# Packing the last 96 gate and up columns of two slabs in each gated layer, with another order of loads at the start

## Chip, cores, metric

One Trainium2 chip, one of its cores. The metric is the device time of one execution, in microseconds. The kernel before takes 395.33 us (median of three runs, 395.28 to 396.86).

## The reference

Four residual layers on x of 2048 tokens by 512 features, bf16: A, B, A, B, each on a layer norm of x, with the same weights in both A and both B.

```python
def _A_ref(x, wqkv, w_phi, wo):            # H = 32 heads of Dh = 16
    q, k, v = split(x @ wqkv)
    pq = einsum("bhsd,hdf->bhsf", q, w_phi); pk = einsum("bhsd,hdf->bhsf", k, w_phi)
    phi_q = concat([softmax(pq), softmax(-pq)]); phi_k = concat([softmax(pk), softmax(-pk)])
    kv = einsum("bhsf,bhsd->bhfd", phi_k, v);  z = einsum("bhsf->bhf", phi_k)
    o = einsum("bhqf,bhfd->bhqd", phi_q, kv) / (einsum("bhqf,bhf->bhq", phi_q, z)[..., None] + 1e-6)
    return heads_joined(o) @ wo

def _B_ref(x, W_gate, W_up, W_down):       # 512 -> 1376 -> 512
    gate = x @ W_gate; up = x @ W_up
    return ((gate * (gate > 0)) * up) @ W_down

x = x + _A_ref(layernorm(x)); x = x + _B_ref(layernorm(x))
x = x + _A_ref(layernorm(x)); x = x + _B_ref(layernorm(x))
```

## The kernel before

**Tiles and slabs.** The 2048 tokens are 16 tiles of 128, or 4 slabs of 512. x stays on the chip (`x_sb`); every layer norm writes a normalized tile, which is transposed into `yT` (features on the partitions, in 4 pieces of 128), by a DMA, or for the first four tiles by TensorE and a copy.

**Attention layer.** w_phi is folded into the query and key weights (`compose_k`, `compose_q`): the wqkv key columns are loaded in four row pieces (wk0 to wk3 below), transposed on TensorE (L514), copied (L518, L520), multiplied with a block-diagonal form of w_phi (`BD`, built by GpSimd at L495 from `phi_c` and `mask8`), and copied to `Wkp` (L524). Then `kv_proj` or `kv_pair` for each tile: keys and values by matmul, two exps on ScalarE, the key sums Zk (L634) and their reciprocal (L636) on VectorE, the division on GpSimd (L639), and `kv_acc`, which adds up phi_k times v over all tiles in banks 0 to 2. `kv_fin` brings this to SBUF; `num` makes each tile's numerator and denominator (L711), divides (VectorE and GpSimd), transposes by DMA, and multiplies with wo (L742).

**Gated layer.** F = 1376 columns are eleven chunks: ten of 128 and one of FLAST = 96. For a group of tiles (`ts`: two tiles, or a slab of four), `glu_up` does per chunk four gate matmuls and four up matmuls (one for each 128 features; n = 256 or 512 tokens stream through a stationary of 128 or 96 columns), L763, then ReLU of the gate by ScalarE into one of three gate buffers (L765), and the product with the up half into one of NHU = 18 buffers of `hT`: by VectorE straight from PSUM (L775), or, for the chunks in `on_act`, through a copy of the up half by ScalarE (L770) and a product from SBUF (L772). `glu_down` (L790) multiplies, for each tile, the eleven chunks of hT with Wd into one bank, the 96-row chunk last, and VectorE adds the result to x (L792). In the first gated layer slabs 2 and 3 go without `on_act`, and their steps are mixed with numerators and the next attention layer's keys; in the last one all chunks are in `on_act`, and slabs 2 and 3 have no other work mixed in.

**Order.** No engine's order is written by hand. The program is a list of operations with what they read and write, an estimated duration, and for DMAs a number of bytes. A planner (`schedule`) places them: at each step the operation that can start first, ties broken by a priority, within a window of operations per engine (24 on GpSimd, 40 on VectorE, 64 on ScalarE, 400 on TensorE). It does so 48 times with different priorities and keeps the order with the shortest end by its own durations. So a changed duration or byte count can alter the order anywhere. Operations with a `boost` (all loads of the start) are first on their queue, in the order in which they are written. On the chip each engine then runs its list in order and waits by semaphores. All matmuls of a PSUM bank and their readers are ordered by the bank (`RP`).

**The start.** SP issues x tile 0, phi, tiles 1 to 3, then (after wk2 has landed, `first`) tiles 4 and 5, 6 and 7, wv, 8 to 11, 12 to 15, and the transposed load of the query weights; ScalarE's queue issues wk0 to wk3. Tiles 0 to 3 are transposed through banks 7, 0, 1 and 0; the key and value banks of layer A0 cycle through 4, 5, 6, 7 (tile 0: 4 and 5, tile 1: 6 and 7). The weights wo, Wg, Wu and Wd are loaded later by SP, after yT of tile 15.

Of the kernel before, what the change touches and what calls it, by code (L numbers as in the profile page):

```python
# [347 lines left out]
ALU = mybir.AluOpType  # L348
# [7 lines left out]
NHU = 18  # L356
# [12 lines left out]
class Kernel:  # L369
# [27 lines left out]
    def alloc(self, E):  # L397
        nc = self.nc

        def sb(name, shape, dt=BF16):  # L400
            t = E(nc.sbuf_tensor(name, [P] + shape, dt))
            setattr(self, name, t)
            return t

        sb("x_sb", [NT, 512])
        sb("yT", [NC, S])
        sb("wv_p", [NC, 512])
        sb("Wqp", [NC, 512])
        sb("Wkp", [NC, 512])
        sb("wo_p", [NC, 512])  # L410
        sb("Wg", [NC, F])
        sb("Wu", [NC, F])
        sb("Wd", [NFC, 512])
        sb("expk", [NT, 2, 512])
        sb("vsb", [NT, NC, 130])
        sb("expq", [NSLAB, NC, 2, 512])
        sb("kvbd", [NG, GW])
        sb("hT", [NHU, 512])
        sb("numbf", [2, NG, GW])
        sb("tsc", [2, 1024])  # L420
        sb("osb", [2, 512])
        sb("oT", [4, NC, 128])
        sb("gate_sb", [3, 512])
        sb("ytile", [4, 512])
        sb("ident", [128])
        sb("mask8", [8])
        sb("mask8t", [8])
        sb("phi_c", [NC, DH])
        sb("stats6", [NT, 6], FP32)
        sb("mv", [NT, 2], FP32)  # L430
        sb("rv1", [NT, 1], FP32)
        sb("rstd", [NT, 1], FP32)
        sb("nmr", [NT, 1], FP32)
        sb("agg", [4, 3], FP32)
        sb("aggw", [2], FP32)
        sb("mhalf", [4, 1], FP32)
        sb("Zk", [2, 64], FP32)
        sb("rZk", [4, 64], FP32)
        sb("zm", [2, 64], FP32)
        sb("zd", [2, 32], FP32)  # L440
        sb("zr", [2, 32], FP32)
        sb("ab", [2, 64])
        self.ps = E(nc.psum_tensor("ps", [P, 8, 512], FP32))
        self.pb = [self.ps[:, i, :] for i in range(8)]
        self.RP = [self.r("pb", i) for i in range(8)]


    def setup(self):
        op, dma, r = self.op, self.dma, self.r
        k = self  # L450
# [16 lines left out]
           [r("tsc", 0)], [r("mask8t")], 200, "mask8 a")  # L467
        op("pool", lambda e: e.affine_select(k.mask8[:], k.mask8t[:], [[16, 8]], ALU.is_ge, 0.0, base=15, channel_multiplier=-1),
           [r("mask8t")], [r("mask8")], 200, "mask8 b")
# [3 lines left out]
        def ldx(t0, t1, after=()):  # L473
            dma("sp", lambda e: e.dma_start(k.x_sb[:, t0:t1, :], xv[:, t0:t1, :]), list(after), [r("x", t) for t in range(t0, t1)], 96000 if t1 == t0 + 1 else (131072 if t0 < 8 else 86000) * (t1 - t0), f"dma x{t0}")
        ldx(0, 1)
        dma("act", (lambda ic: lambda e: e.dma_start(wk_n[:, ic, :], A_wqkv[ic * 128:(ic + 1) * 128, 512:1024]))(0), [], [R_wkn[0]], 96000, f"dma wk0")
        dma("sp", lambda e: e.dma_start(k.phi_c[:], A_w_phi.rearrange("(kc hl) d f -> (hl d) kc f", hl=8)), [], [r("phi_c")], 16384, "dma phi")
        dma("act", (lambda ic: lambda e: e.dma_start(wk_n[:, ic, :], A_wqkv[ic * 128:(ic + 1) * 128, 512:1024]))(1), [], [R_wkn[1]], 96000, f"dma wk1")
        ldx(1, 2)
        dma("act", (lambda ic: lambda e: e.dma_start(wk_n[:, ic, :], A_wqkv[ic * 128:(ic + 1) * 128, 512:1024]))(2), [], [R_wkn[2]], 96000, f"dma wk2")  # L480
        ldx(2, 3)
        dma("act", (lambda ic: lambda e: e.dma_start(wk_n[:, ic, :], A_wqkv[ic * 128:(ic + 1) * 128, 512:1024]))(3), [], [R_wkn[3]], 96000, f"dma wk3")
        ldx(3, 4)
        first = [R_wkn[2]]
        ldx(4, 6, first)
        ldx(6, 8, first)
        dma("sp", lambda e: e.dma_start(k.wv_p[:], wqkv_v[:, :, 1024:1536]), first, [r("wv", ic) for ic in range(NC)], 345000, "dma wv")
        ldx(8, 12, first)
        ldx(12, 16, first)
        o = dma("sp", lambda e: e.dma_start_transpose(WqT, A_wqkv[:, 0:512]), first, R_WqT, 422000, "dma wqT")  # L490
        o.dur = 6400.0
        for j, o in enumerate(self.prog.ops[n0:]):
# [6 lines left out]
           [r("phi_c"), r("mask8")], [R_BD], 1040, "BD")  # L499
# [248 lines left out]
    def glu_up(self, ts, ring, tag, out, on_act=()):  # L748
# [29 lines left out]
        for fc in range(NFC):  # L778
            out.append(lambda fc=fc: step(fc))

# [21 lines left out]
    def emit(self):  # L802
        from itertools import cycle
        self.unit, self.unit_of = 0, {}
# [4 lines left out]
        for t in tiles(0):  # L809
            self.ln(t, "L0", pe_bank=(7, 0, 1, 0)[t], copy_act=True)  # L810
# [23 lines left out]
        for i, piece in enumerate(pieces):  # L834
            piece(self.r("yT", 15 if i < 8 else 15))
        kv(6, 2)
# [7 lines left out]
        for li in (0, 2):  # L844
# [11 lines left out]
            def steps_B(ts, on_act=()):  # L856
                out = []
                self.glu_up(ts, gring, B, out, on_act)
# [6 lines left out]
            def steps_N(ts):  # L865
                return [lambda t=t: N([t]) for t in ts]
# [29 lines left out]
            if not last:  # L896
                mix(steps_B(tiles(2)), steps_N([14, 15]) + steps_K(0))
                mix(steps_B(tiles(3)), steps_K(1) + steps_K(2) + [lambda: self.q_proj(0, mring, "A2")])
# [7 lines left out]
            else:  # L906
                mix(steps_B(tiles(2), HA), [])
                mix(steps_B(tiles(3), HA), [])
# [68 lines left out]
```

## Time and profile before

| what | us |
|---|---|
| median of three runs | 395.33 |
| the profiled execution | 395.28 |
| its span, first to last instruction | 393.6 |

Busy time of the engines in it, us, by stretches of the span:

| stretch | what runs | PE | DVE | ACT | POOL |
|---|---|---|---|---|---|
| 0 to 20 | loads, composed weights, first tiles | 13.21 | 12.37 | 12.55 | 9.65 |
| 20 to 54 | rest of the first keys and values | 31.52 | 31.12 | 27.18 | 32.65 |
| 54 to 75 | queries, first numerators | 19.49 | 16.42 | 18.27 | 8.27 |
| 75 to 225 | first gated layer, mixed with both neighbours | 149.16 | 113.58 | 63.37 | 67.71 |
| 225 to 275 | second attention layer's turn | 48.44 | 38.29 | 36.19 | 24.74 |
| 275 to 375 | second gated layer | 99.47 | 51.02 | 45.65 | 26.09 |
| 375 to 393.6 | its end | 15.93 | 5.29 | 4.45 | 0.00 |

In the lines of the profile, PE is TensorE's matmuls, PEld its weight loads, DVE VectorE, ACT ScalarE, POOL GpSimd, SPq the issuing of DMAs by SyncE. A matmul's duration includes a tail that runs under the next one, so the distance between two starts is its cost in a stream. The granted TensorE clock was 1.00 throughout the span.

### The profile page before, as it was taken

The numbers are of one execution on the slowest core, as the hardware profiler recorded it, in microseconds if no ns is written. First come the engines' busy times: TensorE is split into PE (matmuls) and PEld (weight loads), VectorE is DVE, ScalarE is ACT, GpSimd is POOL, SyncE is SP. The second block draws the span as 40 slices with busy tenths as digits, with TensorE's granted clock in tenths as the row PEclk, the third lists the DMA queues.
The fourth block names the chain that finished last, engine by engine and source line by source line (L and its number), as shares of the span: only waits on it lengthen the run. The fifth ranks groups of instructions, "written<-read, shape, count | busy, mean of one in ns | idle before, by whom it ended". The sixth has DMA issues, their size and how long they took to land.

```text
span 393.6 us, 6346 instructions
## 1 busy us (share of the span) xinstructions
PE 377.2 (96%) x2288; PEld 208.1 (53%) x2331; DVE 268.1 (68%) x547; ACT 207.7 (53%) x389; POOL 169.1 (43%) x284
## 2 busy tenths in 40 slices
PE   4899899999999999999999999989999999999997
PEld 3345464676744444444444457467774454444444
DVE  4799878887757899866756867877775567322322
ACT  4789759743734312543454474985464562454340
POOL 5499934552543373364344543474544152100000
PEclk9999999999999999999999999999999999999999
DMA  6933681322220312301000010142322132100001
GB/s 166 222 68 82 182 305 40 55 53 43 55 40 13 55 41 57 80 14 28 13 13 2 20 36 2 40 68 54 68 55 60 35 51 58 40 2 27 28 13 53
DMA packets 61679, 23.01 MB, mean 58 GB/s; under 512 B 53488, under 2 KB 60624, under 8 KB 61648
## 3 DMA queue, kind: packets, MB, share of 16 engines
q1 hardware_dynamic: 60928, 22.02, 24.6%
q10 hardware_dynamic: 720, 0.59, 0.5%
q8 instruction: 18, 0.29, 0.3%
q14 instruction: 13, 0.11, 0.1%
HBM read 7.91 MB, written 2.10 MB: 25 GB/s over the span
## 4 chain that ended last, share of the span: by engine, by line
PE 84%; DVE 5%; DMA 4%; issue 4%; ACT 1%; SPq 0%; ACTq 0%; POOL 0%; DVEq 0%; POOLq 0%
PE ps L763 39%; PE ps L790 19%; PE ps L622 8%; PE ps L742 6%; PE ps L695 6%; PE ps L711 4%; PE ps L668 3%; DMA x_sb<-in_A_x_dram 2%; DVE rZk L636 1%; DMA yT<-ytile 1%; DVE stats L556 1%; DMA hT<-in_A_wqkv_dram 1%; DVE Zk L634 1%; DVE ytile L599 0%; ACT expq L698 0%
## 5 line engine op out<-in xcount | busy, mean ns | idle before, releaser
L763 PE MATMUL ps<-yT,Wg 128*128 128x512 bf16 (+3 forms) x436 | 125.9, 336 | 1.4 <-ACT expk L770 0.7
L763 PE MATMUL ps<-yT,Wu 128*128 128x512 bf16 (+3 forms) x435 | 123.8, 336 | 0.4
L765 ACT ACTIVATE gate_sb<-ps 128x512 bf16<-128x512 f32 (+3 forms) x110 | 56.2, 512 | 108.3 <-PE ps L763 94.3
L790 PE MATMUL ps<-Wd,hT 128*128 128x512 bf16 (+2 forms) x351 | 104.4, 372 | 0.6
L639 POOL TENSOR_TENSOR expk<-expk,rZk 128x1024 bf16<-128x1024 bf16 (+1 forms) x32 | 59.5, 1882 | 29.6 <-DVE rZk L636 21.0
L763 PEld LDWEIGHTS ps<-yT,Wg 128*128 128x128 bf16 (+1 forms) x440 | 43.7, 100 | 34.3 <-issue 1.3
L763 PEld LDWEIGHTS ps<-yT,Wu 128*128 128x128 bf16 (+1 forms) x440 | 43.8, 100 | 33.3 <-DVE hT L775 0.2
L790 PEld LDWEIGHTS ps<-Wd,hT 128*128 128x128 bf16 (+1 forms) x363 | 35.3, 98 | 36.0 <-DVE x_sb L792 0.4
L772 DVE TENSOR_TENSOR hT<-gate_sb,expk 128x512 bf16<-128x512 bf16 (+3 forms) x73 | 28.9, 396 | 31.3 <-ACT expk L770 30.6
L556 DVE BATCH_NORM_STATS2 stats<-x_sb 128x6 f32<-128x512 bf16 x64 | 42.3, 675 | 7.9 <-DMA x_sb<-in_A_x_dram 7.6
L634 DVE TENSOR_REDUCE Zk<-expk 128x64 f32<-128x1024 bf16 x32 | 37.9, 1202 | 9.3 <-ACT expk L625 9.3
L366 ACT ACTIVATE numbf<-ps 128x432 bf16<-128x432 f32 x64 | 33.1, 541 | 16.5 <-PE ps L711 16.2
L736 POOL TENSOR_TENSOR osb<-tsc 128x512 bf16<-128x512 bf16 x28 | 33.0, 1178 | 20.2 <-DVE tsc L731 18.0
L742 PE MATMUL ps<-wo_p,oT 128*128 128x512 bf16 x122 | 38.1, 379 | 0.7 <-DMA oT<-osb 0.5
L563 POOL TENSOR_SCALAR rv<-mv 128x1 f32<-128x1 f32 (+1 forms) x53 | 12.7, 244 | 56.8 <-DVE mv L558 56.7
L770 ACT ACTIVATE expk<-ps 128x512 bf16<-128x512 f32 (+3 forms) x73 | 36.1, 495 | 0.4 <-PE ps L763 0.2
L698 ACT ACTIVATE expq<-ps 128x1024 bf16<-128x1024 f32 (+1 forms) x40 | 32.2, 866 | 5.6 <-PE ps L695 5.2
L792 DVE TENSOR_TENSOR x_sb<-x_sb,ps 128x512 bf16<-128x512 bf16 (+1 forms) x33 | 21.9, 666 | 19.2 <-PE ps L790 18.9
L625 ACT ACTIVATE expk<-ps 128x512 bf16<-128x512 f32 x44 | 23.9, 595 | 20.9 <-PE ps L622 20.6
L711 PE MATMUL ps<-kvbd,expq 128*128 128x144 bf16 x256 | 34.1, 226 | 0.5 <-ACT numbf L366 0.4
L775 DVE TENSOR_TENSOR hT<-gate_sb,ps 128x512 bf16<-128x512 bf16 (+2 forms) x37 | 22.6, 612 | 16.5 <-PE ps L763 14.4
L695 PE MATMUL ps<-yT,Wqp 128*128 128x512 bf16 x121 | 32.8, 379 | 0.8 <-ACT expq L698 0.5
(73 smaller groups left out, 442.6 us busy)
## 6 DMA issues: line engine op xcount, KB each, us to landing
out_dram<-x_sb SPq DMA_DIRECT2D x15, 128.0 KB, 1.7
Wg<-in_B_W_gate_dram SPq DMA_DIRECT2D x4, 344.0 KB, 4.9
Wu<-in_B_W_up_dram SPq DMA_DIRECT2D x4, 344.0 KB, 5.4
Wd<-in_B_W_down_dram SPq DMA_DIRECT2D x5, 256.0 KB, 7.2
x_sb<-in_A_x_dram SPq DMA_DIRECT2D x2, 512.0 KB, 7.4
yT<-ytile SPq DMA_TRANSPOSE x60, 2.4
x_sb<-in_A_x_dram SPq DMA_DIRECT2D x4, 128.0 KB, 4.6
hT<-in_A_wqkv_dram ACTq DMA_DIRECT2D x4, 128.0 KB, 3.9
```

The lines of the kernel that those rows point to most:

```text
L366: return e.activation(out, in_, ACT.Copy) if hasattr(e, "activation") else e.tensor_copy(out, in_)
L556: op("dve", (lambda t: lambda e: e.bn_stats(k.stats6[:, t, :], k.x_sb[:, t, :]))(t), [r("x", t)], [r("st", t)], 685, f"{tag} stats {t}")
L634: op("dve", lambda e: e.tensor_reduce(k.Zk[:, zb, :], k.expk[:, t, :, :].rearrange("p s (h f) -> p (s h) f", f=16), AX.X, ALU.add), [r("ex ...
L639: op(eng, (lambda s0, s1: lambda e: e.tensor_tensor(k.expk[:, t, s0:s1, :].rearrange("p s (h f) -> p (s h) f", f=16), k.expk[:, t, s0:s1, ...
L695: op("pe", (lambda c, ic, bank: lambda e: e.matmul(k.pb[bank][:], k.Wqp[:, ic, c * 128:(c + 1) * 128], k.yT[:, ic, st * 512:(st + 1) * 512 ...
L711: op("pe", (lambda s, c, j, g0, bank: lambda e: e.matmul(k.pb[bank][:, j * GW:(j + 1) * GW], k.expq[:, st, c, s, tt * 128:(tt + 1) * 128], ...
L736: op(sm, lambda e: e.tensor_tensor(k.osb[:, b, :], k.tsc[:, b, 0:512], k.tsc[:, b, 512:1024], ALU.add), [r("tsc", b)], [r("osb", b)], 418 ...
L742: op("pe", (lambda c, bank: lambda e: e.matmul(k.pb[bank][:], k.oT[:, ob, c, :], k.wo_p[:, c, :], start=(c == 0), stop=(c == NC - 1)))(c, ...
L763: op("pe", (lambda bank, W, ic, fc, Mf: lambda e: e.matmul(k.pb[bank][0:Mf, 0:n], W[:, ic, fc * 128:fc * 128 + Mf], k.yT[:, ic, c0:c0 + n] ...
L765: op("act", (lambda Mf, gb, gs: lambda e: e.activation(k.gate_sb[0:Mf, gs, 0:n], k.pb[gb][0:Mf, 0:n], ACT.Relu))(Mf, gb, gs), [self.RP[gb] ...
L770: op("act", (lambda Mf, ub, tu: lambda e: e.activation(k.expk[0:Mf, tu, 0, 0:n], k.pb[ub][0:Mf, 0:n], ACT.Copy))(Mf, ub, tu), [self.RP[ub] ...
L790: op("pe", (lambda fc, Kf, u, c0, bank, m0, m1: lambda e: e.matmul(k.pb[bank][:, m0:m1], k.hT[0:Kf, u, c0:c0 + 128], k.Wd[0:Kf, fc, m0:m1] ...
```

## The change

Two things. **Packing:** for slabs 2 and 3 of each gated layer, the last 96 gate and 96 up columns are computed from a new tensor `Wr`, which holds, per 128 features, 64 up columns, 64 gate columns, 32 up columns and 32 gate columns. GpSimd fills it once by four copies. `short64` runs the 64 + 64 as one stationary of 128 columns (4 matmuls for each slab). `short32` runs the 32 + 32 as a stationary of 64 columns; slab 2 goes to the lower half of a bank's partitions, slab 3 to the upper half, matmuls alternating (8 matmuls for both slabs, emitted as one operation after slab 2's other steps). ReLU and product run on each part by itself, straight from PSUM; the parts come together in rows 0 to 63 and 64 to 95 of one hT buffer, so `glu_down` is unchanged. Slab 3's buffer is taken when slab 2's halves run.

**The start:** phi is issued first, then tiles 0 to 3; the gate for the later loads is wk3 instead of wk2; tiles 4 to 7 are one load; the planner's byte counts for the loads are larger; tiles 0 and 1 are transposed through bank 7, 2 and 3 through bank 6. `mask8t` and `phi_c` lose their own tensors and lie in `tsc` and `hT`.

```diff
+        sb("Wr", [NC, 192])
-        sb("mask8t", [8])
-        sb("phi_c", [NC, DH])
+        self.mask8t = self.tsc[:, 1, 0:8]
+        self.phi_c = self.hT[:, 13, 0:NC * DH].rearrange("p (c f) -> p c f", c=NC)
...
-            dma("sp", ..., 96000 if t1 == t0 + 1 else (131072 if t0 < 8 else 86000) * (t1 - t0), f"dma x{t0}")
-        ldx(0, 1)
...
-        ldx(3, 4)
-        first = [R_wkn[2]]
-        ldx(4, 6, first)
-        ldx(6, 8, first)
-        dma("sp", lambda e: e.dma_start(k.wv_p[:], wqkv_v[:, :, 1024:1536]), first, ..., 345000, "dma wv")
+            dma("sp", ..., 131072 * (t1 - t0) if t1 > t0 + 1 else 96000, f"dma x{t0}")
+        dma("sp", lambda e: e.dma_start(k.phi_c[:], ...), [], [r("hT", 13)], 16384, "dma phi")
+        for ic in range(NC):
+            dma("act", ..., [], [R_wkn[ic]], 96000, f"dma wk{ic}")
+        for t in range(4):
+            ldx(t, t + 1)
+        first = [R_wkn[3]]
+        ldx(4, 8, first)
+        dma("sp", lambda e: e.dma_start(k.wv_p[:], wqkv_v[:, :, 1024:1536]), first, ..., 524288, "dma wv")
         ldx(8, 12, first)
         ldx(12, 16, first)
-        o = dma("sp", ..., first, R_WqT, 422000, "dma wqT")
-        o.dur = 6400.0
+        o = dma("sp", ..., first, R_WqT, 524288, "dma wqT")
+        o.dur = 7000.0
...
+    def pack_weights(self):
+        op, r, k = self.op, self.r, self
+        for W, nm, o0, o1 in ((k.Wu, "Wu", 0, 128), (k.Wg, "Wg", 64, 160)):
+            for dst, src, n in ((o0, 1280, 64), (o1, 1344, 32)):
+                op("pool", (lambda W, dst, src, n: lambda e: e.tensor_copy(k.Wr[:, :, dst:dst + n], W[:, :, src:src + n]))(W, dst, src, n),
+                   [r(nm, ic) for ic in range(NC)], [r("Wr", dst)], 200 + 4 * n, f"pack {nm} {dst}")
...
-    def glu_up(self, ts, ring, tag, out, on_act=()):
+    def glu_up(self, ts, ring, tag, out, on_act=(), short=0):
...
+        def short64():
+            bank = next(ring)
...
+            for ic in range(NC):
+                op("pe", (lambda ic: lambda e: e.matmul(k.pb[bank][:, 0:n], k.Wr[:, ic, 0:128], k.yT[:, ic, c0:c0 + n], start=(ic == 0), stop=(ic == NC - 1)))(ic), ...)
+            op("act", lambda e: e.activation(k.gate_sb[0:64, gs, 0:n], k.pb[bank][64:128, 0:n], ACT.Relu), ...)
+            op("dve", lambda e: e.tensor_tensor(k.hT[0:64, u, 0:n], k.gate_sb[0:64, gs, 0:n], k.pb[bank][0:64, 0:n], ALU.mult), ...)
+
+        def short32():
+            bank = next(ring)
+            t2 = list(range(ts[-1] + 1, ts[-1] + 1 + len(ts)))
+            us = [self.unit_of[ts[0], NFC - 1][0], self.new_short(t2)]
+            self.short_of[t2[0]] = us[1]
+            def mm(e):
+                for ic in range(NC):
+                    for v in range(2):
+                        last = e.matmul(k.pb[bank][v * 64:v * 64 + 64, 0:n], k.Wr[:, ic, 128:192], k.yT[:, ic, c0 + v * n:c0 + v * n + n], start=(ic == 0), stop=(ic == NC - 1), skip_group_check=True)
+                return last
+            op("pe", mm, ..., 4 * du + 190, f"{tag} Wr2 {ts[0]}")
+            for v, u in enumerate(us):
+                gs = u % 3
+                op("act", ... e.activation(k.gate_sb[64:96, gs, 0:n], k.pb[bank][v * 64 + 32:v * 64 + 64, 0:n], ACT.Relu) ...)
+                op("dve", ... e.tensor_tensor(k.hT[64:96, u, 0:n], k.gate_sb[64:96, gs, 0:n], k.pb[bank][v * 64:v * 64 + 32, 0:n], ALU.mult) ...)
+
-        for fc in range(NFC):
+        for fc in range(NFC - 1 if short else NFC):
             out.append(lambda fc=fc: step(fc))
+        if short:
+            out.append(short64)
+        if short == 2:
+            out.append(short32)
...
-            self.ln(t, "L0", pe_bank=(7, 0, 1, 0)[t], copy_act=True)
+            self.ln(t, "L0", pe_bank=(7 if t < 2 else 6), copy_act=True)
...
+        self.pack_weights()
         kv(6, 2)
...
-                mix(steps_B(tiles(2)), steps_N([14, 15]) + steps_K(0))
-                mix(steps_B(tiles(3)), steps_K(1) + steps_K(2) + [lambda: self.q_proj(0, mring, "A2")])
+                mix(steps_B(tiles(2), (), 2), steps_N([14, 15]) + steps_K(0))
+                mix(steps_B(tiles(3), (), 1), steps_K(1) + steps_K(2) + [lambda: self.q_proj(0, mring, "A2")])
...
-                mix(steps_B(tiles(2), HA), [])
-                mix(steps_B(tiles(3), HA), [])
+                mix(steps_B(tiles(2), HA, 2), [])
+                mix(steps_B(tiles(3), HA, 1), [])
```

## The prediction

> **What bounds the kernel now.** Four views, in this order: the page's busy shares, the busy time by stretches, the chain of waits of the first 45 us, and the single shapes of the lines that the change touches.
>
> ```profile
> PE 377.2 (96%) x2288; PEld 208.1 (53%) x2331; DVE 268.1 (68%) x547; ACT 207.7 (53%) x389; POOL 169.1 (43%) x284
> ```
>
> By stretches (start:end, length, busy us and instructions of PE, PEld, DVE, ACT, POOL, then clock, DMA share, GB/s):
>
> ```profile
> 20.00:30.00 10.00, 9.50 (x66) 4.98 (x66) 10.00 (x14) 8.78 (x13) 9.59 (x14) 1.00 0.36 72
> 30.00:40.00 10.00, 9.89 (x69) 5.50 (x70) 10.00 (x15) 9.03 (x12) 10.00 (x6) 1.00 0.38 82
> 40.00:50.00 10.00, 8.18 (x61) 4.63 (x61) 8.09 (x11) 7.09 (x11) 10.00 (x6) 1.00 0.72 202
> ...
> 150.00:175.00 25.00, 24.89 (x116) 11.57 (x116) 19.91 (x41) 10.90 (x20) 11.59 (x19) 1.00 0.25 50
> ...
> 200.00:225.00 25.00, 24.89 (x116) 11.50 (x117) 17.64 (x25) 11.38 (x21) 11.29 (x10) 1.00 0.03 6
> ...
> 325.00:350.00 25.00, 24.89 (x115) 11.40 (x116) 11.18 (x25) 10.66 (x20) 3.59 (x8) 1.00 0.15 37
> ```
>
> The kernel has two regimes. Until some 54 us VectorE and GpSimd set the pace: both are full from 20 to 40 us, and TensorE has 1.8 us without work in the ten after that. In the gated layers TensorE is busy 24.89 of 25 us, and no other engine is near that: there a TensorE slot saved is time saved, and work added elsewhere costs nothing until it delays TensorE. The start's pace comes from this chain (start, length, what):
>
> ```profile
> 1.73 4.75 DMA hT<-in_A_wqkv_dram
> ...
> 6.49 0.38 SPq L474
> ...
> 7.95 7.04 DMA x_sb<-in_A_x_dram
> ...
> 17.52 2.97 DVE stats L556 x5
> 20.50 1.19 DVE Zk L634 x2
> ...
> 41.90 3.29 DMA yT<-ytile
> ```
>
> The third piece of wqkv (wk2) lands at 6.48 us and lets SP issue the later tiles; tiles 8 to 11 go out at 7.95 and land at 14.99; from there VectorE runs without a pause to the last normalized tile, which TensorE awaits at 45.2. VectorE had waited 2.59 us for those tiles.
>
> **The change, part by part.** *1. Fewer matmul slots.* In slabs 2 and 3 of a gated layer the last 96 columns cost 2 x (4 gate + 4 up) = 16 matmuls. The timeline gives their slot:
>
> ```profile
> 349.58 0.38 PE L763 MATMUL ps<-yT,Wg 128*96 128x512 bf16 x1
> 349.80 0.38 PE L763 MATMUL ps<-yT,Wu 128*96 128x512 bf16 x1
> 350.01 0.38 PE L763 MATMUL ps<-yT,Wg 128*96 128x512 bf16 x1
> 350.23 0.38 PE L763 MATMUL ps<-yT,Wu 128*96 128x512 bf16 x1
> ```
>
> Start to start is 0.65/3 = 0.216 us although each lasts 0.379: 0.163 is tail, hidden under the next. So 16 slots are 3.45 us a layer. After: 64 + 64 columns in one stationary, 4 matmuls in each slab, 8 ordinary slots, 1.73 us. The 32 + 32 columns are 8 matmuls of 64 columns, alternating between two halves of the array. No row shows halves working at once, so I bound it. Perfect pairs: 4 slots, 0.86 us. Pairs with an exposed tail when the halves come into use and when they go: 0.86 + 2 x 0.163 = 1.19. No overlap, with the two tails: 1.73 + 0.33 = 2.05. A tail after each matmul: 8 x 0.379 = 3.03. Against the 1.73 that these 8 replace, the gain per layer is 0.86, 0.54, -0.33 or -1.30; for two layers 1.73, 1.07, -0.65 or -2.61. I take 1.07: the halves write different partitions and read different columns of yT, so no data orders them, and the tail is what a row shows for an array that is not refilled at once.
>
> The weight loads could break the pairs. A 128-column load takes 98 ns, a 96-column one 123 (below); two per pair make 0.20 to 0.25 us against a slot of 0.216, so at worst (0.246 - 0.216) x 4 x 2 = 0.24 us in all, kept for the range.
>
> ```profile
> L763 PEld LDWEIGHTS ps<-yT,Wg 128*96 128x96 bf16 x40 | 4.8, 123 | 3.1
> L765 ACT ACTIVATE gate_sb<-ps 96x512 bf16<-96x512 f32 x6 | 3.6, 593 | 5.3 <-PE ps L763 4.5 <-DVE tsc L731 0.8
> L775 DVE TENSOR_TENSOR hT<-gate_sb,ps 96x512 bf16<-96x512 bf16 x2 | 1.4, 684 | 1.4 <-PE ps L763 1.4
> ```
>
> Two rules of the Trainium skill speak against the edit. "TensorEngine Tiling (Array Packing)", Key Properties, says that a change of tiling mode drains the array; the tail of 0.163 us is my row for a drain, and without that rule the sum would gain 1.73 instead of 1.07. "TensorE: Matmul & The Clock Gate", Part 3, gives three column tiles a speed-up of 2.38; scaled to two tiles (an estimate from that page) it is 1.59, so 8 matmuls in 1.09 us, and a gain of 1.28 before drains; the same rows that I have show no such pair.
>
> *2. More evacuation.* Both ReLU and product now run on the 64-row and the 32-row part separately: 4 of each per layer where there were 2. A narrow tile is no cheaper (593 ns at 96 rows, 598 at 128). First layer: ACT + 2 x 0.593 = 1.19 us, DVE + 2 x 0.684 = 1.37. Second layer: four ReLUs replace two ReLUs and two copies of the up half, ACT even; DVE 4 x 0.684 - 2 x 0.416 = + 1.90. I cost all of it at nothing: in those stretches DVE has at least 5 us of every 25 free, ACT 13. If the cover went, down's eleventh matmul would wait for ReLU and product after the halves, 1.28 us; ten matmuls of the same tile, 2.16 us, stand before it.
>
> *3. Packing the weights.* Four copies on GpSimd, once. The nearest rows are the 64-element copy of 0.24 us (L503) and the 512-element product of 1.04 (L495); at 256 and 128 elements, 0.24 to 1.04 each, 1.0 to 4.2 us in all, some 1.8 in between. Wg and Wu, issued up to 47.8 us, land by 54.0; GpSimd then has a hole:
>
> ```profile
> 52.51 1.50 POOL L639 TENSOR_TENSOR expk<-expk,rZk 128x512 bf16<-128x512 bf16 x1 [0.94 <-DVE rZk L636]
> 61.41 0.31 POOL L722 TENSOR_TENSOR zm<-numbf 128x64 f32<-128x64 bf16 x1 [7.41 <-DVE numbf L366]
> ```
>
> 7.4 us hold all four: cost nothing. Put ahead of the last key normalization instead, they would wait for the weights, and kv_acc, kv_fin and every numerator behind that: up to 1.5 us and the copies.
>
> *4. The start goes over to another order.* Phi is issued ahead of tile 0: phi some 0.45 us earlier, tile 0 as much later. Neither decides: GpSimd's product with phi ends at 5.45, but the weight columns behind it wait for wk2 anyway; tile 0's statistics end at 4.3, and its tile is written at 8.0. What decides is SP's queue. The gate moves from wk2 (6.48) to wk3, whose transposes start at 7.20: + 0.72. Tiles 4 to 7 are one issue instead of two: - 0.48. Then wv, tiles 8 to 11, 12 to 15 and the transposed load follow + 0.24 later, and landings between + 0.24 and, if the queue's bytes simply slide, + 0.72. VectorE has no slack behind them: + 0.48, the middle. Below nothing too: a planner that expects tiles 8 to 11 later (524288 bytes for wv instead of 345000) may put the first two key sums (1.2 us each) into VectorE's 2.59 us wait, up to - 2.4.
>
> *5. Banks.* Tiles 2 and 3 are transposed through bank 6, tiles 0 and 1 through bank 7. Bank 6 is also where tile 1's keys go, so these now wait for tile 3's copy, which ended at 17.84 while the keys of tile 1 were done by 12.8. Zero, because tile 1's key sum runs only at 21.6; the rival below prices the rest.
>
> Sum, against the profiled execution (span 393.6, 395.28 in all; the median is 395.33): 395.28 - 1.07 + 0.48 = **394.7 us**.
>
> **Rivals.** *The start is filled better.* The key sums move into the 2.59 us wait. For it: the exps of tiles 0 and 1 end at about 13.0 and at 13.96, so the sums could run. Against: tiles 4 to 7 arrive later too, which narrows the hole. With one sum gained (1.2) and perfect pairs: 395.28 - 1.73 + 0.48 - 1.2 = 392.8.
>
> *The halves do not overlap and each matmul shows its tail.* Place: the 8 half matmuls of each layer. Price: + 2.61, so 395.28 + 2.61 + 0.48 = 398.4. It is slower by 0.5% once a half matmul costs over (1.73 + (2.03 - 0.48)/2)/8 = 0.31 us (397.31, the upper bound of no change below, is 2.03 above 395.28). For it: the weight load runs longer for narrow stationaries. Against: the 96-column matmuls keep the 0.216 slot.
>
> *Tile 1's keys stick behind bank 6.* If ScalarE keeps its order, its exps of tile 1 slide from 12.9 (four run in a row from 11.89 to 13.96) to 17.84 + 4 x 0.216 = 18.7, 5.8 us, of which its idle time from 10 to 20 us (2.1) swallows part: 3.7 us of everything behind it, 395.28 - 1.07 + 3.7 = 397.9. It decides when tile 3's copy ends after some 16 us. Against: the planner sees this dependency and can bring tile 3 forward.
>
> *The change does nothing here:* no overlap, tails only at the ends, 395.28 + 0.65 + 0.48 = 396.4, inside "no change".
>
> **How the numbers follow.** A measurement of this kernel tells 0.5%, 1.98 us, from no change; around 395.33 that is 393.35 to 397.31. Forecast 0.46 and the idle change 0.10 lie inside; better start 0.20, below; tails 0.10 and bank 6 0.14, above. So faster 0.20, same 0.56, slower 0.24. The range goes from 392.8 (perfect pairs and one sum gained, with the 0.24 of slow loads still inside) to 397.9 (the price of bank 6): beyond lie the tails' rival, 0.10, and the far halves of the other two, some 0.10.
>
> **What would show it.** Right: in slabs 2 and 3 four 64-column matmuls start in some 0.43 us, not 0.86; TensorE's busy time falls by about 1 us in the gated layers; the pack copies stand between 54 and 61 us; tiles 8 to 11 land at 15.2 to 15.7; the last key normalization ends near 54.5. Wrong: half matmuls 0.216 or 0.38 apart; key sums ahead of the statistics of tile 8; exps of tile 1 after 17 us; a GpSimd wait on Wu; or a stretch after 75 us in which TensorE falls under 24.8 of 25.

## The result, and the profile after

The changed kernel takes 393.66 us (median of six runs, 393.24 to 394.04) beside 395.35 for the kernel before: ratio 0.9951, 95% interval 0.9935 to 0.9967. Repeated later, twelve runs gave 394.99 (394.04 to 396.38) beside 395.34: ratio 0.9991, interval 0.9978 to 1.0003. In some executions of these kernels the granted TensorE clock was 0.987 to 0.996 instead of 1.00, and in six of the eight kernels that had such executions they took 1.3 to 2.2 us longer at the median; where that matters, the median of the executions at 0.999 or 1.00 is given as "at full clock". At full clock the repeat took 394.44 us (seven runs) beside 395.33. So the change is between 0.1 and 0.5% faster, within what a measurement of this kernel tells from no change. The profiled execution took 393.43 us, span 391.7, which is 1.9 below the span before.

The page's busy shares, and busy time by stretches (columns as before):

```profile
PE 375.1 (96%) x2290; PEld 205.4 (52%) x2331; DVE 270.7 (69%) x551; ACT 208.3 (53%) x391; POOL 169.9 (43%) x288
```

```profile
20.00:30.00 10.00, 8.09 (x58) 4.37 (x58) 10.00 (x13) 8.41 (x12) 8.92 (x13) 1.00 0.44 57
30.00:40.00 10.00, 9.89 (x72) 5.62 (x73) 10.00 (x13) 7.97 (x11) 10.00 (x6) 1.00 0.35 79
40.00:50.00 10.00, 8.13 (x58) 4.39 (x57) 7.89 (x10) 7.02 (x12) 10.00 (x6) 1.00 0.72 224
...
200.00:225.00 25.00, 24.89 (x115) 11.35 (x116) 17.33 (x28) 11.29 (x20) 11.95 (x11) 1.00 0.08 16
...
300.00:325.00 25.00, 24.45 (x129) 12.00 (x131) 15.71 (x33) 11.96 (x24) 9.23 (x18) 1.00 0.18 39
325.00:350.00 25.00, 24.89 (x119) 11.17 (x119) 10.92 (x25) 11.44 (x20) 2.41 (x6) 1.00 0.17 41
```

From 200 to 225 and from 325 to 350 us TensorE is as full as before, 24.89 of 25 us, and no wait of TensorE names the added ReLUs, products or copies: they are hidden. From 300 to 325 us it is not: 24.45 instead of 24.84, with a wait for a product of a slab that is not packed:

```profile
322.77 0.39 PE L840 MATMUL ps<-Wd,hT 96*128 96x512 bf16 x1 [0.39 <-DVE hT L776]
```

At the start VectorE is as full as before, but GpSimd has 1.1 us free between 20 and 30 us, and TensorE 1.9, where before they had 0.4 and 0.5. That is a place where the change lost part of what its start had won.

The timeline of TensorE around the set of halves in the last gated layer, and the shapes of the new lines:

```profile
348.48 0.81 PE L767 MATMUL ps<-yT,Wu 128*128 128x512 bf16 x3
349.22 1.05 PE L807 MATMUL ps<-yT,Wr 128*64 128x512 bf16 x8
350.20 0.39 PE L840 MATMUL ps<-Wd,hT 128*128 128x512 bf16 x1
```

```profile
L814 DVE TENSOR_TENSOR hT<-gate_sb,ps 32x512 bf16<-32x512 bf16 x4 | 2.7, 682 | 2.0 <-ACT gate_sb L812 2.0
...
L812 ACT ACTIVATE gate_sb<-ps 32x512 bf16<-32x512 f32 x4 | 2.4, 588 | 0.5 <-DVE hT L776 0.5
L807 PE MATMUL ps<-yT,Wr 128*64 128x512 bf16 x16 | 2.1, 385 | 0.0
...
L807 PEld LDWEIGHTS ps<-yT,Wr 128*64 128x64 bf16 x16 | 0.7, 109 | 1.3 <-issue 0.8
```

Three matmuls start at 348.48, 0.216 apart, the last at 348.91, so the set could start at 349.13 (348.91 + 0.216). It starts at 349.22, 0.09 later, and the next matmul stands at 350.20: 0.98 us for eight, of which four slots of 0.216 are 0.86. With the entry the set costs some 1.08 us, five slots, where eight ordinary ones would cost 1.73. Narrow tiles are not cheaper for the other engines: 588 ns for a ReLU of 32 rows, 682 for a product.

The chain of waits at the start, and the issue of tiles 8 to 15 by SP:

```profile
1.86 4.12 DMA x_sb<-in_A_x_dram
...
10.78 2.38 DVE stats L552 x4
...
15.72 4.16 DVE stats L552 x7
...
39.70 1.10 DVE ytile L593
...
43.61 3.44 DMA yT<-ytile
```

```profile
7.20 1.06 SPq L475 DMA_DIRECT2D x_sb<-in_A_x_dram  x2
```

Before, the chain held the transfer of tiles 8 to 11 (7.04 us, to 14.99). Now it holds tile 0's transfer and then VectorE and GpSimd: tiles 8 to 11 are issued at 7.20 instead of 7.95, and nothing waits for them. VectorE's and GpSimd's timelines show what took the place of that wait (columns: start, length; in brackets idle time before it):

```profile
13.36 1.18 DVE L630 TENSOR_REDUCE Zk<-expk 128x64 f32<-128x1024 bf16 x1
14.46 0.68 DVE L552 BATCH_NORM_STATS2 stats<-x_sb 128x6 f32<-128x512 bf16 x1
...
21.32 1.96 DVE L593 TENSOR_SCALAR ytile<-x_sb,rstd,nmr 128x512 bf16<-128x512 bf16 x1
```

```profile
21.21 1.93 POOL L635 TENSOR_TENSOR expk<-expk,rZk 128x1024 bf16<-128x1024 bf16 x1
...
23.90 1.93 POOL L635 TENSOR_TENSOR expk<-expk,rZk 128x1024 bf16<-128x1024 bf16 x1 [0.55 <-DVE rZk L632]
25.78 1.05 POOL L577 TENSOR_TENSOR rstd<-rv,mhalf 128x4 f32<-128x4 f32 x1
...
51.52 2.77 POOL L635 TENSOR_TENSOR expk<-expk,rZk 128x512 bf16<-128x512 bf16 x2 [1.39 <-DVE rZk L632]
54.24 0.63 POOL L748 COPY Wr<-Wg 128x256 bf16<-128x256 bf16 x2
```

The planner put tile 0's key sum into the former wait, so GpSimd divides from 21.21 on. Before, it divided from 23.45 to 51.58 without a break:

```profile
23.45 28.13 POOL L639 TENSOR_TENSOR expk<-expk,rZk 128x1024 bf16<-128x1024 bf16 x15
```

Now layer-norm operations and waits stand between the divisions, and the last one ends at 54.29 (51.52 + 2.77) against 54.01. A lead of 2.24 us became a delay of 0.28. Some of the lead was kept even so: the first matmul of the gated layers starts 0.98 us earlier than before. Before, then after:

```profile
74.95 0.27 PE L763 MATMUL ps<-yT,Wg 128*128 128x256 bf16 x1 [0.19 <-DMA yT<-ytile]
```

```profile
73.97 0.27 PE L767 MATMUL ps<-yT,Wg 128*128 128x256 bf16 x1 [0.17 <-DMA yT<-ytile]
```

So of the 1.9 us of span 0.98 come ahead of this matmul and 0.9 behind it.

### The profile page after: what moved, and what is told of

It is laid out like the page before. It is cut to its first block, busy times and chain, and to the rows that moved or that the text cites. A ratio compares the mean times of both kernels' runs of the same rounds, so it can differ in the third digit from the quotient of the medians.

```text
span 391.7 us, 6354 instructions
## 1 busy us (share of the span) xinstructions
PE 375.1 (96%) x2290; PEld 205.4 (52%) x2331; DVE 270.7 (69%) x551; ACT 208.3 (53%) x391; POOL 169.9 (43%) x288
## 4 chain that ended last, share of the span: by engine, by line
PE 81%; DVE 7%; issue 4%; DMA 3%; POOL 2%; ACT 2%; SPq 0%; DVEq 0%; POOLq 0%
PE ps L767 36%; PE ps L840 19%; PE ps L618 8%; PE ps L691 6%; PE ps L738 6%; PE ps L707 4%; PE ps L664 2%; DVE stats L552 2%; ACT expq L694 2%; DMA yT<-ytile 2%; DVE Zk L630 1%; DVE rZk L632 1%; POOL rstd L560 1%; DVE ytile L593 1%; DMA x_sb<-in_A_x_dram 1%
## 5 line engine op out<-in xcount | busy, mean ns | idle before, releaser
L767 PE MATMUL ps<-yT,Wu 128*128 128x512 bf16 (+3 forms) x419 | 117.3, 334 | 0.5 <-DVE zr L722 0.2
L767 PE MATMUL ps<-yT,Wg 128*128 128x512 bf16 (+3 forms) x415 | 114.9, 334 | 1.2 <-DMA oT<-osb 0.6
L769 ACT ACTIVATE gate_sb<-ps 128x512 bf16<-128x512 f32 (+3 forms) x106 | 53.0, 509 | 102.6 <-PE ps L767 89.7
L840 PE MATMUL ps<-Wd,hT 128*128 128x512 bf16 (+3 forms) x355 | 104.4, 373 | 0.9 <-DVE hT L776 0.4
L767 PEld LDWEIGHTS ps<-yT,Wu 128*128 128x128 bf16 (+1 forms) x424 | 42.0, 99 | 31.9 <-ACT expk L774 0.4
L767 PEld LDWEIGHTS ps<-yT,Wg 128*128 128x128 bf16 (+1 forms) x424 | 41.4, 99 | 32.0 <-issue 1.0
L774 ACT ACTIVATE expk<-ps 128x512 bf16<-128x512 f32 (+3 forms) x71 | 35.0, 495 | 8.4 <-PE ps L767 8.1
L691 PE MATMUL ps<-yT,Wqp 128*128 128x512 bf16 x123 | 34.0, 379 | 0.9 <-ACT expq L694 0.6
L560 POOL TENSOR_TENSOR rstd<-rv,mhalf 128x1 f32<-128x1 f32 (+1 forms) x53 | 30.9, 587 | 2.6
L618 PE MATMUL ps<-Wkp,yT 128*128 128x512 bf16 x85 | 28.1, 379 | 2.9 <-DMA yT<-ytile 1.8
```

What stands on the lines that cost most here:

```text
L618: op("pe", (lambda ic, bank, W: lambda e: e.matmul(k.pb[bank][:], k.yT[:, ic, t * 128:(t + 1) * 128], W[:, ic, :], start=(ic == 0), stop=( ...
L691: op("pe", (lambda c, ic, bank: lambda e: e.matmul(k.pb[bank][:], k.Wqp[:, ic, c * 128:(c + 1) * 128], k.yT[:, ic, st * 512:(st + 1) * 512 ...
L767: op("pe", (lambda bank, W, ic, fc, Mf: lambda e: e.matmul(k.pb[bank][0:Mf, 0:n], W[:, ic, fc * 128:fc * 128 + Mf], k.yT[:, ic, c0:c0 + n] ...
L769: op("act", (lambda Mf, gb, gs: lambda e: e.activation(k.gate_sb[0:Mf, gs, 0:n], k.pb[gb][0:Mf, 0:n], ACT.Relu))(Mf, gb, gs), [self.RP[gb] ...
L774: op("act", (lambda Mf, ub, tu: lambda e: e.activation(k.expk[0:Mf, tu, 0, 0:n], k.pb[ub][0:Mf, 0:n], ACT.Copy))(Mf, ub, tu), [self.RP[ub] ...
L840: op("pe", (lambda fc, Kf, u, c0, bank, m0, m1: lambda e: e.matmul(k.pb[bank][:, m0:m1], k.hT[0:Kf, u, c0:c0 + 128], k.Wd[0:Kf, fc, m0:m1] ...
```

## The experiments

**The packing alone.** Loads, gate, byte counts and banks as before; the packing stays.

```diff
-        first = [R_wkn[3]]
-        ldx(4, 8, first)
+        first = [R_wkn[2]]
+        ldx(4, 6, first)
+        ldx(6, 8, first)
...
-            self.ln(t, "L0", pe_bank=(7 if t < 2 else 6), copy_act=True)
+            self.ln(t, "L0", pe_bank=(7, 0, 1, 0)[t], copy_act=True)
```

> The packing alone, on the start of before (its loads, gates, byte counts and banks). Theory A (the halves overlap, and the packing is where the time comes from): the set of 8 half matmuls takes about 1.07 us from its slot to the next matmul's, two layers gain 1.3 us, so 394.0 us. Theory B (the other order of the start brought the time, the packing little): 395.3 us, no change.

Measured: 394.95 us, ratio 0.9991 (0.9975 to 1.0007); span 393.3. The set takes the same 0.99 us, but the span fell by 0.3 and not by the 1.29 of the slots. TensorE's timeline shows a wait that the kernel before does not have there:

```profile
106.30 0.38 PE L772 MATMUL ps<-yT,Wg 128*128 128x512 bf16 x1
107.66 0.39 PE L743 MATMUL ps<-wo_p,oT 128*128 128x512 bf16 x1 [0.98 <-DMA oT<-osb]
```

(The weight load of one more matmul, which has no record, falls into it, so some 0.9 us are lost.) It lies some 60 us ahead of the first packed matmul: the planner ordered the first gated layer anew, and one output tile comes too late. This wait does not close the sum by itself, for the first gated matmul also starts 0.68 us earlier than before, at 74.27. From there to the end of the span this kernel takes 319.0 us, where the kernel before takes 318.6: the slots, and 0.4 us more, are lost to waits and order behind it.

**The new start alone.** No packing; all of the start as changed.

```diff
-                mix(steps_B(tiles(2), HA, 2), [])
-                mix(steps_B(tiles(3), HA, 1), [])
+                mix(steps_B(tiles(2), HA), [])
+                mix(steps_B(tiles(3), HA), [])
```

> The other start alone, without packing: all eleven chunks as before, and the planner orders anew. Theory A: the start is worth the rest, 0.3 to 0.5 us, so 394.9 us. Theory B: nearly the whole gain, 393.7 us. The prediction's own term for the start, + 0.48, would give 395.8 us.

Measured: 391.9 us, ratio 0.9915 (0.9897 to 0.9934), span 389.7: 3.9 less than before, more than either theory allowed. GpSimd's timeline:

```profile
20.37 1.93 POOL L634 TENSOR_TENSOR expk<-expk,rZk 128x1024 bf16<-128x1024 bf16 x1
...
25.55 25.75 POOL L634 TENSOR_TENSOR expk<-expk,rZk 128x1024 bf16<-128x1024 bf16 x14
```

Here the divisions run without a break from 25.55 and end at 51.30, 2.7 us ahead of before. The loads are those of the changed kernel; the order is not. So the two halves of the change do not add up: one gives 0.3 in the span, the other 3.9, both together 1.9.

**Do the halves run side by side?** Two kernels. In the first, the four matmuls of the lower half are listed ahead of the four of the upper; its planned order is otherwise that of the changed kernel.

```diff
-                for ic in range(NC):
-                    for v in range(2):
+                for v in range(2):
+                    for ic in range(NC):
```

> The changed kernel with the 8 half matmuls in another sequence: four of the lower half, then four of the upper, so that none can run beside one of the other half; the planner's order is the same, instruction for instruction outside of these 8. Theory A: the set goes from 1.07 to about 1.73 + 0.2 = 1.93 us, 0.86 us more in each of two layers, so 395.4 us. Theory B (no true overlap, or a set that does not matter): within 0.3 us of the changed kernel, 393.7 us.

Measured: 394.85 us, ratio 0.9994 (0.9974 to 1.0015); span 393.2. The expected 1.93 us failed:

```profile
350.70 1.06 PE L807 MATMUL ps<-yT,Wr 128*64 128x512 bf16 x8
351.69 0.39 PE L840 MATMUL ps<-Wd,hT 128*128 128x512 bf16 x1
```

The set still takes 0.99 us. By the records of the single matmuls, the second start follows the first by 14 ns. The records do not name the half; but two matmuls of one half stand 0.216 us or more apart (next run), so the second start must be that of the first matmul of the upper half, although it is listed fifth. So this was no test of overlap; the next one is. It puts both slabs on the lower half, in two banks.

```diff
-            bank = next(ring)
+            bank, bank2 = next(ring), next(ring)
+            bb = (bank, bank2)
...
-                        last = e.matmul(k.pb[bank][v * 64:v * 64 + 64, 0:n], ...)
+                        last = e.matmul(k.pb[bb[v]][0:64, 0:n], ...)
```

> The changed kernel with all 8 half matmuls on the same half of the array: slab 3's results go to the lower partitions of a second bank. Theory A (the halves work at once): the set goes from 1.08 us to 8 x 0.216 + 0.19 = 1.92 us from its slot to the next matmul, + 1.7 us in all. Rival (matmuls of 64 columns are simply twice as fast, on whichever half): 1.08 us as before.

Measured: 395.69 us, ratio 1.0009 (0.9988 to 1.0029); span 393.6.

```profile
350.32 1.91 PE L808 MATMUL ps<-yT,Wr 128*64 128x512 bf16 x8
352.17 0.39 PE L841 MATMUL ps<-Wd,hT 128*128 128x512 bf16 x1
```

1.85 us, and 0.09 at the entry: 1.94 instead of 1.08. The two halves of the array save 0.86 us per layer by running at once, and the rival, that 64 columns are simply twice as fast, falls. Of the 1.7 us expected in all, 1.2 to 1.5 show: from the first gated matmul to the end this kernel takes 319.2 us, the changed kernel 317.7 and, repeated, 318.0.

**Is it the order?** The planner's random start was changed and nothing else, in the kernel before and in the changed one, and the changed kernel was run again.

```diff
-        rng = random.Random(1)
+        rng = random.Random(2)
```

> The kernel before with another seed for the noise with which the planner compares its 48 orders: nothing else changes. It shows how much the order alone moves the time. Theory A: under 0.5 us, 394.9 to 395.8 us, so that terms of 1.3 us can be told from it. Theory B: over 1 us either way, and then no single comparison of two planned kernels tells what an edit is worth.

> The changed kernel with another seed for the planner's noise. Its list for VectorE in the first 50 us is then nearly that of the run with the start alone (the normalization of tile 14 stands before the key sums of tiles 10 and 11, not after that of tile 10); the packing is the same. Theory O (the packing gains its 1.3 us, and the changed kernel lost 3 us to a worse order of the first keys): the start alone has a ratio of 0.9915, less 1.3 us is 0.988, 390.6 us. Theory P (the packing itself costs what the start gained, by its extra ReLUs, products and buffers): 0.991 to 0.996, no better than the start alone.

> The changed kernel once more, beside the next three on the same chip. Its ratio to the kernel before should again be near 0.9951; more than 0.003 off would say that chips or runs differ by as much as the terms that are told apart here.

The kernel before stayed where it was: 395.16, ratio 0.9998 (0.9985 to 1.001). This says nothing of what an order is worth: in the two traces TensorE, VectorE, ScalarE and GpSimd each run the same operations on the same names and shapes in the same sequence, so the other random start ended in the same order. It shows the scatter of one program instead: the profiled spans are 393.6 and 392.8. The changed kernel did get another order and went to 391.8 us (391.43 to 391.96), ratio 0.9907 (0.9893 to 0.9921), span 389.9: the fastest kernel of the study, level with the new start alone. That is neither theory's time: the order was worth about the 3 us of Theory O, but the packing shows little on top of it (from the first gated matmul to the end, 317.9 us against 318.3 with the start alone). Its GpSimd:

```profile
18.29 1.93 POOL L635 TENSOR_TENSOR expk<-expk,rZk 128x1024 bf16<-128x1024 bf16 x1
...
24.48 27.64 POOL L635 TENSOR_TENSOR expk<-expk,rZk 128x1024 bf16<-128x1024 bf16 x15
```

Its divisions end at 52.12, 2.2 us ahead of the changed kernel's. Same instructions, same loads, another order: 1.8 us of span, and beside the repeat, on the same chip and at full clock, 2.6 us (391.8 and 394.44). The repeat of the changed kernel had the changed kernel's sequence there, but tile 0's key sum had to wait 0.62 us for its exps and began at 14.14 instead of 13.36; its divisions ended at 55.32, and its span was 393.0: one order scatters by over 1 us too. Its ratio is 0.004 off the first one, more than the 0.003 that its expectation allowed, so single terms of about 1 us cannot be read from one pair of times.

**Which part of the start?** In the kernel before, first the planner's byte counts alone, then the banks alone.

```diff
-            dma("sp", ..., 96000 if t1 == t0 + 1 else (131072 if t0 < 8 else 86000) * (t1 - t0), f"dma x{t0}")
+            dma("sp", ..., 131072 * (t1 - t0) if t1 > t0 + 1 else 96000, f"dma x{t0}")
...
-            self.ln(t, "L0", pe_bank=(7, 0, 1, 0)[t], copy_act=True)
+            self.ln(t, "L0", pe_bank=(7 if t < 2 else 6), copy_act=True)
```

(wv, the transposed load and its duration as in the change; the last two lines belong to the second kernel.)

> The kernel before with only the planner's numbers for the loads changed to those of the changed kernel (bytes of x, wv, wqT, and the issue time of wqT); no load, gate or bank changes. The planner then puts the key sums of tiles 0 and 1 before the statistics of tile 8. Theory O: the wait of 2.59 us is used, GpSimd starts its divisions 2 to 3 us earlier, and 1 to 3 us are gained, 392.3 to 394.3 us. Rival (the gate, the merged load or the banks bring it): 395.3 us, no change.

> The kernel before with only the banks of the first four transposes changed to those of the changed kernel (7, 7, 6, 6). Theory O: the key sum of tile 0 still stands after the statistics of tile 15, so nothing is gained, 394.8 to 395.8 us. The prediction's rival (keys of tile 1 stuck behind bank 6): 397 to 398 us. The other rival (banks bring the gain): 392 to 394 us.

Byte counts: 395.18 us, ratio 0.9982 (0.9969 to 0.9996). The numbers that only the planner sees did move key sums into the wait, and GpSimd began 4.7 us earlier, at 18.75 instead of 23.45. It still finished later, at 55.46:

```profile
18.75 1.93 POOL L639 TENSOR_TENSOR expk<-expk,rZk 128x1024 bf16<-128x1024 bf16 x1
...
40.00 3.86 POOL L639 TENSOR_TENSOR expk<-expk,rZk 128x1024 bf16<-128x1024 bf16 x2 [1.07 <-DVE rZk L636]
44.94 10.52 POOL L639 TENSOR_TENSOR expk<-expk,rZk 128x1024 bf16<-128x1024 bf16 x6 [1.07 <-ACT expk L656]
```

Banks: 397.35 us, ratio 1.0039 (1.0019 to 1.0058). That is the time that was expected if bank 6 delays tile 1's keys, but the trace gives it another cause. At full clock it is 395.92 (four of the twelve, 395.41 to 396.10), and the profiled span is 0.6 above that before. TensorE, ScalarE and VectorE:

```profile
16.55 1.04 PE L622 MATMUL ps<-Wkp,yT 128*128 128x512 bf16 x4 [0.95 <-ACT yT L610]
```

```profile
17.62 1.08 ACT L625 ACTIVATE expk<-ps 128x512 bf16<-128x512 f32 x2 [0.43 <-PE ps L622]
```

```profile
20.62 2.34 DVE L634 TENSOR_REDUCE Zk<-expk 128x64 f32<-128x1024 bf16 x2
```

Tile 1's keys wait for the copy out of bank 6, and its exps run at 17.62 instead of some 12.9. But the key sums that read them run only from 20.62, where they ran from 20.41 before, so the delay is nearly all swallowed: GpSimd's first division starts at 23.57 (before 23.45), the last ends at 53.31 (54.01), and the first gated matmul starts 0.86 us earlier, at 74.09. The loss lies behind it, 320.1 us to the end instead of 318.6, with this as the longest wait:

```profile
95.11 0.39 PE L742 MATMUL ps<-wo_p,oT 128*128 128x512 bf16 x1 [1.65 <-DMA oT<-osb]
```

In the changed kernel the planner had brought the copy forward, to end at 12.34, and the exps run at 14.12: the mechanism is there, and that order escaped most of it.

**Normalization forced ahead.** The normalizations of the first layer get the highest priority, in the changed kernel, in the start alone and in the kernel before, in order to compare all three at a like order.

```diff
+            for o in prog.ops:
+                if o.boost == 0.0 and o.name.startswith(("L0 apply", "L0 ag", "L0 rv1", "L0 rstd", "L0 nmr")):
+                    o.boost = 1e6
```

> The changed kernel with a priority for the first layer norm's small operations (statistics' sums, reciprocal roots, and the normalization of each tile) over the key work on VectorE and GpSimd; packing and loads are the same. Theory O (the changed kernel gives its better start back because VectorE's normalizations come late and are held while GpSimd divides: 0.41 us alone, up to 1.96 us there, and TensorE then waits 1.5 and 1.8 us for yT): those waits go and 391 to 392 us result, a ratio of 0.989 to 0.992. Rival (the loss is the loads' arrival, which varies by run): 393.5 to 395 us.

> The same priority on the other start without packing. Its distance to the kernel of the line above is what the packing is worth with the start's order nearly equal. Theory A: 0.9 to 1.3 us slower than that kernel (1.29 us of slots, less 0.4 us of new waits for hT). Rival P (the packing's slots are lost again in its longer evacuation): within 0.3 us of it.

> The kernel before with the same priority and nothing else. Theory O: the order of the first keys is worth 1 to 2.5 us by itself, whatever the loads: 393 to 394.3 us. Rival (the new gate and loads are needed for it): 395.3 us.

Measured: 394.92 us, ratio 1.0001 (0.9979 to 1.0023); 397.25, ratio 1.0053 (1.0036 to 1.007); 397.5, ratio 1.0055 (1.0036 to 1.0075). As a cure it failed: no kernel came near 392. In the changed kernel GpSimd now waits for the first reciprocal:

```profile
23.60 1.93 POOL L635 TENSOR_TENSOR expk<-expk,rZk 128x1024 bf16<-128x1024 bf16 x1 [2.05 <-DVE rZk L632]
...
31.99 23.72 POOL L635 TENSOR_TENSOR expk<-expk,rZk 128x1024 bf16<-128x1024 bf16 x13 [1.40 <-DVE rZk L632]
```

What the three do show is the packing: at this order, with and without it, 394.92 against 397.25, spans 393.0 and 395.2. The slots are 1.29 of these 2.2; the rest, some 0.9, is order again. The first gated matmul agrees with this: it starts at 75.36 and 76.23, 0.87 apart, and from there to the end the two kernels take 317.7 and 319.0 us, 1.3 apart.

**What the orders have in common.** Two numbers go with the span over all kernels: the end of the last division, and the start of the first gated matmul. To compare, the last column adds the packing's saved slots to the span of the packed kernels (1.29; where both slabs run on one half the set costs 0.21 more than eight slots in each layer, so 0.43 is taken off).

| kernel | first division starts | last one ends | first gated matmul | from it to the end | span | span without packing's share |
|---|---|---|---|---|---|---|
| new start alone | 20.37 | 51.30 | 71.42 | 318.3 | 389.7 | 389.7 |
| changed, other random start | 18.29 | 52.12 | 72.06 | 317.9 | 389.9 | 391.2 |
| before, other random start | 22.59 | 53.14 | 74.07 | 318.7 | 392.8 | 392.8 |
| before, banks | 23.57 | 53.31 | 74.09 | 320.1 | 394.2 | 394.2 |
| packing alone | 22.77 | 53.33 | 74.27 | 319.0 | 393.3 | 394.6 |
| before | 23.45 | 54.01 | 74.95 | 318.6 | 393.6 | 393.6 |
| changed | 21.21 | 54.29 | 73.97 | 317.7 | 391.7 | 393.0 |
| both slabs on one half | 21.50 | 54.77 | 74.45 | 319.2 | 393.6 | 393.2 |
| changed, halves listed apart | 21.14 | 55.09 | 74.75 | 318.4 | 393.2 | 394.5 |
| changed, repeated | 21.77 | 55.32 | 74.99 | 318.0 | 393.0 | 394.3 |
| before, byte counts | 18.75 | 55.46 | 75.55 | 318.3 | 393.9 | 393.9 |
| changed, normalization ahead | 23.60 | 55.71 | 75.36 | 317.7 | 393.0 | 394.3 |
| start, normalization ahead | 24.06 | 56.30 | 76.23 | 319.0 | 395.2 | 395.2 |
| before, normalization ahead | 20.56 | 57.39 | 77.04 | 318.7 | 395.7 | 395.7 |

The correlation of the last column with the end of the divisions is 0.84 (0.8 us of span per us), with the first gated matmul 0.92 (1.0 us per us), with the first division's start only 0.45. The first gated matmul differs by 5.6 us between the kernels, the rest of the span by 2.4: most of what the orders are worth is decided ahead of the gated layers and carried through them. Of the packing's 1.29 us some 0.7 is left behind that matmul, by medians (318.0 in the six profiles with overlapping halves, 318.7 in the seven without packing). An early first division was worth little where the stream behind it had holes. This is a correlation over 14 spans, some of one program, not a proof that the end of the divisions alone sets the time.

## Why the prediction was right, and where it was not

The time, 393.66 beside 394.7, lies in the range and inside "no change". The sum behind it held in one term and failed in the other, and that the time fell into the range was in part luck: the same kernel in another order took 391.8, below it. In the profile the start gave 0.98 us instead of costing 0.48, and 0.9 came behind it, the 1.29 of the slots less some 0.4 that went elsewhere: 395.28 - 0.98 - 0.9 = 393.4, where 393.43 was measured. Two of the prediction's own signs of being wrong came: a key sum ahead of the statistics of tile 8 (13.36 and 14.46), and stretches after 75 us with TensorE under 24.8 of 25 (24.65 from 75 to 100 us, 24.45 from 300 to 325, both 24.84 before).

**Slots.** Right in kind: the halves overlap, an entry and an exit are exposed. The mis-sized part is the tail: 0.163 each was taken from the ordinary matmul; measured are 0.09 at the entry and 0.12 from there on (0.98 less 0.86; by the single records 0.02 of it lies behind the first pair and 0.10 at the exit), together one slot. So the gain is three slots per layer, 0.65, and 1.29 in all, not 0.54 and 1.07. The loads of 64 columns take 109 ns, inside the bounds of 98 and 123, and did not break the pairs. The rival of a tail after each matmul, and the change that does nothing, fell with the 0.98 us. "TensorE: Matmul & The Clock Gate", Part 3, in the Trainium skill, has the speed-up from which the prediction estimated 1.09 us for the eight; the runs show 0.98, and 1.08 with the entry.

**Evacuation and packing copies at nothing.** Right, as far as TensorE's waits show: none names them. The copies took 1.39 us where 1.8 were estimated, from 54.24 to 55.46 in the hole after the divisions.

**The start at + 0.48: the step that failed.** It said that the gate "moves from wk2 (6.48) to wk3, whose transposes start at 7.20: + 0.72", and added that to the old landing times. With phi first and tile 0 behind it the pieces of wk landed sooner: the gate opened at 6.23 (at 5.93 to 6.47 in the seven other profiles with these loads), so tiles 8 to 11 were issued 0.75 us earlier. At the median 6.6 us of the three merged loads they would land at 13.8, 1.2 before the old 14.99; VectorE, busy with a key sum until 14.46, did not wait. The old wait of 2.59 us was gone.

**"The start is filled better", given 0.20,** came in part and was taken back. One key sum did go into the wait. The prediction then let that lead run through to the end; instead the new order put layer-norm operations and waits between the divisions (0.55, 1.05, 1.39 in the lines above), and the normalizations that TensorE needs next were held while GpSimd divided: four of the five in this stretch took 1.96, 1.23, 1.23 and 1.18 us, where an unhindered one takes 0.41. In the kernel before, four are held as well, but for less: 0.94 and three times 0.78. TensorE then waits for a normalized tile 1.52 us up to 25.79 and 1.81 up to 47.10; before, there was one such wait, 1.77 up to 45.24, so the first is new and the second comes 1.86 us later. Of a lead of 2.24 us, 0.98 was left at the first gated matmul; in the repeat, which starts it at 74.99, nothing was left. That the holding is what costs the lead was not shown: where the normalizations were put ahead, only one stayed held in the changed kernel (1.92), and its time was no better.

**Bank 6.** Place and mechanism were right where the banks alone were changed: the exps of tile 1 stood at 17.62, forecast 18.7. The price of 3.7 us was wrong: the first division came 0.12 us later, and the first gated matmul not later at all. What the prediction gave as its reason for nothing, that the key sum runs late anyway, is what this trace shows. The reason against the rival, that the planner can bring the copy forward, was right for the changed kernel.

**What the sum left out.** It took the old order as given and slid it. Edits as small as a byte count, a bank or an operation 60 us later made the planner pick another order, and in the one pair where only the order differs it is worth 2.6 us, more than the packing. Open remains which edit of the start gives the 0.85% that it wins alone: byte counts alone gave 0.2%, banks alone won nothing, and the gate, the order of phi and the merged load were not tried singly. Nor was it shown by an edit that touches only the end of the divisions that this end sets the time.

## What to carry to other kernels

Where a planner picks the order, one run of an edit measures the edit and one draw of an order: value the edit by its slots in the trace, and time it over several orders before keeping or dropping it. Follow an early gain to the end of the stream that it feeds; a first operation 2 to 5 us earlier was worth little here when the last one ended no sooner. And after any edit try other orders of the same kernel: here another random start gave the changed kernel 0.7% (394.44 to 391.8 us), more than the edit had given in its first order; for the kernel before it ended in the same order and gave nothing.

## What the runs showed of the hardware

The two halves of the array run side by side whichever way they are listed: 3 ns between the partners' starts when they alternate, 14 ns when, as inferred above, the second half's first matmul stands fifth in the list. "TensorEngine Tiling (Array Packing)", Key Properties, in the Trainium skill, says that tiles load and multiply independently of each other; these runs agree, and its drain on a change of mode agrees with the 0.09 us at the entry and 0.10 at the exit, which stand there also with all eight on one half.

VectorE's normalization beside GpSimd's division is held, not slowed by a share: the one that started at 21.32 ended at 23.28, just after the division that had started at 21.21 and ended at 23.14; without a division beside it, it takes 0.41 (the one at 15.30). "SBUF — State Buffer", Who interferes with whom, in the Trainium skill, says that the two engines share a pair of ports which the first to start keeps for its whole instruction; this trace agrees.
